# Keys x values with the values stationary in column halves, key sums by quarters of ones, and three transposes per pair

## The chip, the cores and the metric

The kernel runs on one core of a Trainium2 chip. Its time is the device time of one execution in microseconds (us); of several executions the median counts. The core's engines work side by side and wait for one another through semaphores: TensorE (PE; its weight loads are listed apart as PEld), VectorE (DVE), ScalarE (ACT), GpSimd (POOL) and SyncE (SP), which here issues most DMAs. All arithmetic is on 32-bit floats.

## The reference

A linear attention over 2 batches, 8 heads, 576 positions and 64 columns per head is followed by two blocks of wide layers. Only the attention matters here:

```
phi(x):  proj = x @ w_phi                        # 64 -> 128 features
         proj -= max(abs(proj), per row)
         return concat(exp(proj), exp(-proj))    # 256 features
q_p, k_p = phi(q), phi(k)
kv  = einsum('bhsf,bhsd->bhfd', k_p, v)          # 256 x 64 per head
z   = sum(k_p, over s)                           # 256 per head
num = einsum('bhsf,bhfd->bhsd', q_p, kv)
den = einsum('bhsf,bhf->bhs', q_p, z) + 1e-06
out = num / den
```

The result, 1152 rows of 512 columns, goes through `(x @ w_a) * (x @ w_b) @ w_out` and then through four weighted branches `relu(x @ w1[e]) @ w2[e]`.

## The kernel before, in words

The order of all work is written out by hand, as a loop over slots. In each slot every engine gets a few instructions, in program order, and an engine never passes one of its own that waits.

**Tiles.** Heads are handled in pairs, four pairs per batch. A tile is 128 rows of keys or queries of one pair; 576 rows are four full tiles and 64 rows more, so the last 64 rows of two neighbouring pairs share one mixed tile ("m"). A batch has 18 tiles, taken two at a time: nine items. There are 18 key items (slots 0 to 17) and then 18 query items (slots 18 to 35), and the loop runs some slots beyond.

**A key item** passes through three steps. `stage_proj` (L182) runs in the item's own slot: six products on PE give the projection `pj`, VectorE takes the row maxima `mx` and subtracts them (`r`, L193 and L195), ScalarE takes both exponentials (`kp`, L201 and L202). `stage_kv` (L205) runs three slots later, right after the projection of that slot. So in slots 3 to 20 PE's order is: six products of the projection, then the kv stage of the item three slots back.

**The kv stage.** For each tile and each of two heads and two signs of the exponent, 128 features of the keys are the stationary side (`lhsT`), and 128 columns are streamed: 64 columns of that head's values and 64 columns of ones, which give the key sums `z`. The tile `v` holds ones between the values of the two heads of each pair, filled by GpSimd (L142); the values are loaded around them in two DMAs per 128 rows (L151 and L155). A full tile is four products, a mixed tile eight, each over 64 rows. The sums of one pair stand in one PSUM tile `kv` of tag `nd`; when a pair is finished, VectorE (batch 0, L232) or ScalarE (batch 1, L234) copies them to `kvz`, features on the partitions.

**The query items** go through `stage_rt` (L239): four transposes on PE, exponentials on ScalarE. From slot 27 on, `stage_num` (L279) multiplies them with 32-column pieces of `kvz`: first the denominators (k = 0), then the values. `pj` and `rt` share a ring of four PSUM tiles, `num` uses the tag `nd` like `kv`.

**Around it.** Between these, ScalarE, VectorE and GpSimd prepare the weights of the later layers (`begin`, `middle`, `parts`, one step per slot from slot 5), and GpSimd and ScalarE split inputs into two parts (`xp`, L94 and L95). The rest of the kernel, from about 106 us on, is long runs of products on PE. Nothing of that is touched. `later(slot, fn)` puts a call into the list `todo`, which is emptied at the end of each slot's attention work.

Of the kernel before, what the change touches and what calls it, by code (L numbers as in the profile page):

```python
# [9 lines left out]
F32 = mybir.dt.float32  # L10
# [6 lines left out]
B, H, S, D = 2, 8, 576, 64  # L17
NP = H // 2
# [30 lines left out]
def tile_linear_attention_then_mlps(ctx, tc, qT, kT, v, w_phi, wab, wout, w12, probs, out):  # L49
    nc = tc.nc  # L50
    PSUM = bass.MemoryType.PSUM

    const = ctx.enter_context(tc.tile_pool(name="const", bufs=1, side="left"))
# [7 lines left out]
    ident = const.tile([128, 128], F32, name="ident")  # L61
    pr = const.tile([128, NTB * 3, E], F32, name="pr")
    psm = const.tile([128, NTB * 3, 1], F32, name="psm")

    hh_p = ctx.enter_context(tc.tile_pool(name="hh", bufs=1, side="left"))
    od_p = ctx.enter_context(tc.tile_pool(name="od", bufs=1, side="left"))
# [2 lines left out]
    k_p = tc.alloc_tile_pool(name="k", bufs=1, side="left")  # L69
    r_p = tc.alloc_tile_pool(name="r", bufs=1, side="right")  # L70
    nd_p = tc.alloc_tile_pool(name="nd", bufs=2, space=PSUM)
# [9 lines left out]
    with tc.manual_schedule():  # L81
# [6 lines left out]
        nc.vector.memset(wbp.bitcast(F32)[64:128, :, 0:128], 0.0)  # L88

        nc.vector.memset(psm, 0.0)  # L90
        nc.scalar.activation(out=psm, in_=psm, func=AF.Exp)

        def two_parts(hi, lo, src, eng):
# [44 lines left out]
        vt = {}  # L138

        def alloc_v(b):  # L140
            t = k_p.tile([128, 5, NP, 192], F32, tag="v", name="v", bufs=2)
            nc.gpsimd.memset(t[:, :, :, 64:128], 1.0)  # L142
            vt[b] = t

        def load_v(b, st):

            rows = v[b, st * 128:min(S, (st + 1) * 128)]
            n = rows.shape[0]
            for lo in range(0, 128, n):
                o = vt[b][lo:lo + n, st].rearrange("p a c -> p (a c)")  # L150
                nc.sync.dma_start(  # L151
                    out=o[:, 128:128 + 3 * 192].rearrange("p (a c) -> p a c", c=192)[:, :, 0:128],
                    in_=rows[:, 1:H - 1, :].rearrange("s (a h) d -> s a (h d)", h=2),
                )
                nc.sync.dma_start(  # L155
                    out=o.rearrange("p (a c) -> p a c", c=64)[:, 0:4 * NP - NP:3 * NP - 1, :],
                    in_=rows[:, 0:H:H - 1, :],
                )

        def tiles_of_batch():  # L160
            seq = []
# [9 lines left out]
        for kind in "kq":  # L171
            for b in range(B):
                for g in range(9):
                    items.append((kind, b, g, seq[2 * g:2 * g + 2]))

        st_r = {}
        st_kp = {}
        kv_ps = {}
        kvz_t = {}
# [25 lines left out]
        def stage_kv(i):  # L205
            kind, b, g, ts_ = items[i]
            kp = st_kp[i]
            done = []
            for j, t in enumerate(ts_):
                if t[0] == "m":  # L210
                    parts = [(t[1], 4, 0, 64, False, True), (t[2], 4, 64, 128, True, False)]
                else:
                    first, last = t[1] == 0, t[1] == 3
                    parts = [(t[0], t[1], 0, 128, first and t[0] % 2 == 0, last and t[0] % 2 == 1)]
                for p, st, lo, hi, first, last in parts:
                    if first:
                        kv_ps[b, p] = nd_p.tile([128, 2, 512], F32, tag="nd", name="kv")
                for h in range(2):
                    for s in range(2):
                        for p, st, lo, hi, first, last in parts:  # L220
                            c = 256 * h + 128 * s
                            nc.tensor.matmul(  # L222
                                out=kv_ps[b, p][:, 0, c:c + 128],
                                lhsT=kp[lo:hi, 2 * j + h, s, :],
                                rhs=vt[b][lo:hi, st, p, 64 * h:64 * h + 128],
                                start=first and h + s == 0, stop=last, skip_group_check=True,
                            )
                done += [(b, p) for p, st, lo, hi, first, last in parts if last]
            for b, p in done:
                t = kvz_all[:, b * NP + p]  # L230
                if b == 0:
                    nc.vector.tensor_copy(t, kv_ps.pop((b, p))[:, 0])  # L232
                else:
                    nc.scalar.copy(t, kv_ps.pop((b, p))[:, 0])  # L234
                kvz_t[b, p] = t.rearrange("p (h s f) -> p h s f", h=2, s=2)

        kvz_all = hh_p.tile([128, B * NP, 512], F32, tag="hh", name="kvz")

        def stage_rt(i):  # L239
            kind, b, g, ts_ = items[i]  # L240
# [38 lines left out]
        def stage_num(qp, kvz, k):  # L279
            t = nd_p.tile([128, 2, 512], F32, tag="nd", name="num")  # L280
            for i in range(2):
                for s in range(2):
                    for n in range(4):
                        h = n % 2
                        c = 64 * (1 - h) if k == 0 else 64 * h + 32 * (k - 1)
                        nc.tensor.matmul(  # L286
                            out=t[32 * n:32 * n + 32, i, 0:HT],
                            lhsT=kvz[n // 2][:, h, s, c:c + 32],
                            rhs=qp[n // 2][:, s, h, HT * i:HT * i + HT],
                            start=(s == 0), stop=(s == 1), tile_position=(0, 32 * n),  # L290
                        )
            return t
# [483 lines left out]
        load_chunk(0)  # L776
        load_chunk(1)
        alloc_v(0)
        load_v(0, 0)
        load_v(0, 1)  # L780
        split_x(0, nc.vector)
        high, low = ([wbp[D * g:D * g + D, k, 128 * g:128 * g + 128] for g in range(2)] for k in range(2))
# [4 lines left out]
        hi, lo = xpart[0]  # L787
# [3 lines left out]
        for st in range(2, 5):  # L791
            load_v(0, st)
# [5 lines left out]
            nc.vector.reciprocal(out=psm, in_=psm)  # L798
            nc.vector.tensor_tensor(out=pr, in0=pr, in1=psm.to_broadcast([128, NTB * 3, E]), op=ALU.mult)

        todo = {}

        def later(slot, fn, *a):
            todo.setdefault(slot, []).append((fn, a))

        def num(slot, b, half):
            pairs = [(b, 2 * half + k) for k in range(2)]
            qp = [qp_t.pop(bp) for bp in pairs]
            kvz = [kvz_t[bp] for bp in pairs]
            den = stage_den(stage_num(qp, kvz, 0))  # L810
            later(slot + 1, first, slot + 1, b, half, qp, kvz, den)

        def first(slot, b, half, qp, kvz, den):
            t = stage_num(qp, kvz, 1)
            rb = stage_rc(den)
            later(slot + 1, second, slot + 1, b, half, qp, kvz, rb, t)

        def second(slot, b, half, qp, kvz, rb, t0):
            t1 = stage_num(qp, kvz, 2)
            later(slot + 1, stage_xparts, b, 2 * half, stage_x(t0, rb))  # L820
            later(slot + 1, third, slot + 1, b, half, rb, t1)
# [9 lines left out]
        for slot in range(NI + 9):  # L831
            if slot < NI:
                kind, b, g, ts_ = items[slot]
# [12 lines left out]
            i = slot - 3  # L846
            if 0 <= i < NK:
                stage_kv(i)
            i = slot - 4
# [6 lines left out]
            if slot == 2:  # L856
                for _ in range(2):
                    load_raw()
                alloc_v(1)
                make_identity(nc, ident)  # L860
# [19 lines left out]
        for jt in order:  # L880
# [3 lines left out]
            j, tp = jt  # L884
# [65 lines left out]
```

## Time and profile before

| | us |
|---|---|
| median of 3 runs | 718.07 (717.93 to 718.54) |
| the profiled execution | 718.9 |
| its span in the trace | 717.1 |
| PE busy in the span | 709.8 |
| VectorE, GpSimd, ScalarE busy | 424.9, 309.7, 300.8 |

PE is at work almost without a break, and the chain of work that ended last runs over PE for 93% of the span. How much time a step is worth is therefore read from PE's timeline, from the start of one group to the start of the next: PE's instructions are pipelined, so the durations of neighbours overlap. The column "x16" gives the number of recorded passes; a product of 32-bit floats is recorded as two passes, a product of the projection (in a faster 32-bit form) and a transpose as one. The granted clock of PE is 1.00 in every stretch read here.

### The profile page before, as it was taken

The page shows a single profiled execution, that of the slowest core. Times are in us where ns is not written, and L with a number is a line of the kernel's source. Part 1 is how long each engine was busy: PE and PEld are TensorE (multiplying, and loading weights), DVE is VectorE, ACT ScalarE, POOL GpSimd, SP SyncE. Part 2 cuts the span into 40 slices and gives each one's busy share as a digit, 9 for nine tenths or more (in the row PEclk, how much of TensorE's full clock was granted, in tenths as well). Part 3 has the DMA queues.
Part 4 walks back from the last instruction along what each step waited for, and adds up shares of the span by engine and source line. Part 5 has one row for each costly group of instructions (what it writes and reads, how often), then busy time and mean ns, then how long its engine had stood idle before and what let it go on. Part 6 is the DMA issues. An engine that isn't in the chain of part 4 may idle for free.

```text
span 717.1 us, 12721 instructions
## 1 busy us (share of the span) xinstructions
PE 709.8 (99%) x4946; PEld 651.5 (91%) x4946; DVE 424.9 (59%) x715; ACT 300.8 (42%) x614; POOL 309.7 (43%) x294
## 2 busy tenths in 40 slices
PE   9999999999999999999999999999999999999997
PEld 8997669999999999999898989898989888888886
DVE  6879875575777764554555545554545454545454
ACT  6766665455444342233552423242324242424221
POOL 4597564244455435212555343534344334434200
PEclk9999999999999999999999999999999999999999
DMA  6775122222333330012122111211111111100003
GB/s 193 186 206 155 47 62 73 74 87 81 101 103 89 103 90 1 30 30 89 52 66 59 30 41 49 59 31 47 43 59 30 53 36 59 30 30 0 1 1 133
DMA packets 52221, 48.60 MB, mean 68 GB/s; under 512 B 8576, under 2 KB 44096, under 8 KB 52160
## 3 DMA queue, kind: packets, MB, share of 16 engines
q1 hardware_dynamic: 49344, 45.26, 21.5%
q0 software_dynamic: 2592, 2.36, 1.5%
q8 instruction: 39, 0.64, 0.4%
q14 instruction: 22, 0.18, 0.1%
q10 hardware_dynamic: 224, 0.16, 0.1%
HBM read 45.40 MB, written 2.36 MB: 67 GB/s over the span
## 4 chain that ended last, share of the span: by engine, by line
PE 93%; ACT 2%; DVE 2%; DMA 1%; SPq 1%; issue 1%; ACTq 0%; DVEq 0%
PE acc L740 9%; PE acc L739 9%; PE acc L738 9%; PE ab L658 6%; PE ab L660 6%; PE ab L659 6%; PE X L582 5%; PE X L583 5%; PE X L584 5%; PE kv L222 4%; PE num L286 3%; PE acc L689 3%; PE acc L690 3%; PE acc L688 3%; PE Z L582 2%; PE Z L583 2%
## 5 line engine op out<-in xcount | busy, mean ns | idle before, releaser
L748 DVE SCALAR_TENSOR_TENSOR oacc<-acc,pr,oacc 128x512 f32<-128x512 f32 (+1 forms) x136 | 101.5, 746 | 116.5 <-PE acc L740 116.5
L95 POOL TENSOR_TENSOR w<-wx,w 128x512 fp32r<-128x512 f32 x68 | 89.8, 1321 | 144.8 <-ACT w L94 144.8
L95 POOL TENSOR_TENSOR wc<-wt,wc 128x512 fp32r<-128x512 f32 (+1 forms) x48 | 70.1, 1487 | 113.4 <-ACT wc L94 113.4
L740 PE MATMUL acc<-w,hhb 128*128 128x512 f32 x290 | 114.2, 394 | 0.0
L658 PE MATMUL ab<-xh,w 128*128 128x288 f32 x384 | 113.5, 296 | 0.0
L739 PE MATMUL acc<-w,hhb 128*128 128x512 f32 x290 | 113.4, 391 | 0.0
L660 PE MATMUL ab<-xh,w 128*128 128x288 f32 x384 | 113.1, 295 | 0.0
L659 PE MATMUL ab<-xl,w 128*128 128x288 f32 x384 | 113.1, 294 | 0.0
L738 PE MATMUL acc<-w,hhb 128*128 128x512 f32 x290 | 112.8, 389 | 0.0
L582 PE MATMUL X<-xc,wc 128*128 128x288 f32 x256 | 77.1, 301 | 1.4 <-ACT h L587 1.4
L706 ACT ACTIVATE hhb<-h 128x288 fp32r<-128x288 f32 x64 | 36.2, 566 | 98.4 <-DVE h L590 98.4
L583 PE MATMUL X<-xc,wc 128*128 128x288 f32 x256 | 75.7, 296 | 0.0
L584 PE MATMUL X<-xc,wc 128*128 128x288 f32 x256 | 75.4, 295 | 0.0
L658 PEld LDWEIGHTS ab<-xh,w 128*128 128x128 f32 x384 | 72.0, 188 | 1.4 <-issue 1.4
L659 PEld LDWEIGHTS ab<-xl,w 128*128 128x128 f32 x384 | 72.0, 188 | 0.0
L660 PEld LDWEIGHTS ab<-xh,w 128*128 128x128 f32 x384 | 72.0, 188 | 0.0
L587 ACT ACTIVATE h<-X 128x288 f32<-128x288 f32 x64 | 26.0, 406 | 104.6 <-PE X L584 104.4
L740 PEld LDWEIGHTS acc<-w,hhb 128*128 128x128 f32 x290 | 54.4, 188 | 14.1 <-DVE hhb L707 2.9
L707 DVE SCALAR_TENSOR_TENSOR hhb<-h,hhb 128x288 fp32r<-128x288 f32 x64 | 40.5, 633 | 43.1 <-ACT hhb L706 43.1
L427 POOL TENSOR_TENSOR wx<-wx,rn 128x512 uint32<-128x512 uint32 x36 | 46.4, 1289 | 45.4 <-DVE wx L424 45.3
L739 PEld LDWEIGHTS acc<-w,hhb 128*128 128x128 f32 x290 | 54.4, 188 | 8.4
L738 PEld LDWEIGHTS acc<-w,hhb 128*128 128x128 f32 x290 | 54.5, 188 | 7.7
(105 smaller groups left out, 1614.1 us busy)
## 6 DMA issues: line engine op xcount, KB each, us to landing
raw<-in_wab SPq DMA_DIRECT2D x192, 64.0 KB, 2.1
wt<-in_w SPq DMA_DIRECT2D x64, 128.0 KB, 2.4
wx<-in_w SPq DMA_DIRECT2D x32, 256.0 KB, 3.1
raw<-in_wout SPq DMA_DIRECT2D x12, 512.0 KB, 3.7
xp<-in_qT POOLq DMA_DIRECT2D x18, 128.0 KB, 3.4
xraw<-in_qT SPq DMA_DIRECT2D x6, 384.0 KB, 3.4
out<-oacc SPq DMA_DIRECT2D x8, 256.0 KB, 2.0
xraw<-in_kT SPq DMA_DIRECT2D x5, 384.0 KB, 3.9
```

The lines of the kernel that those rows point to most:

```text
L95: eng.tensor_tensor(out=lo, in0=src, in1=hi.bitcast(F32), op=ALU.subtract)
L427: nc.gpsimd.tensor_tensor(out=x, in0=x, in1=r, op=ALU.add)
L582: nc.tensor.matmul(out=ps, lhsT=whi, rhs=xhi, start=first and a == 0, stop=False, skip_group_check=True)
L583: nc.tensor.matmul(out=ps, lhsT=whi, rhs=xlo, start=False, stop=False, skip_group_check=True)
L584: nc.tensor.matmul(out=ps, lhsT=wlo, rhs=xhi, start=False, stop=a == 1, skip_group_check=True)
L658: nc.tensor.matmul(out=t, lhsT=whi, rhs=hi, start=(c == 0), stop=False)
L659: nc.tensor.matmul(out=t, lhsT=whi, rhs=lo, start=False, stop=False)
L660: nc.tensor.matmul(out=t, lhsT=wlo, rhs=hi, start=False, stop=(c == KD - 1))
L738: nc.tensor.matmul(out=acc, lhsT=hi, rhs=whi, start=f == 0, stop=False)
L739: nc.tensor.matmul(out=acc, lhsT=hi, rhs=wlo, start=False, stop=False)
L740: nc.tensor.matmul(out=acc, lhsT=lo, rhs=whi, start=False, stop=f == 1)
L748: nc.vector.scalar_tensor_tensor(out=o, in0=acc, scalar=sc, in1=o, op0=ALU.mult, op1=ALU.add)
```

## The change

- **Loading.** `v` becomes a plain tile of whole rows, 512 columns. There is one DMA where there were two, and the fills of ones on GpSimd go. A small tile `ones` (128 x 32) is filled once.
- **kv stage.** The two sides swap. For each tile and head the 64 value columns are stationary, and the 256 features of the keys are streamed. The result stands on 64 partitions: head 0 on partitions 0 to 63, head 1 on 64 to 127 (`tile_position=(lo, 64 * h)`). The key sums are four products with `ones` as the stationary side, 32 columns wide, each in its own quarter of the columns (`tile_position=(lo, c)`), with 128 features streamed. Two pairs share one PSUM tile, one bank each.
- **Transposes.** The sums now have the features along the free side. When two pairs are finished (four times in all, in slots 7, 11, 16 and 20), ScalarE copies their 768 columns to `kt`; in the next slot `turn` transposes them on PE in six pieces, back into the same PSUM tile; in the slot after that `keep` copies them to `kvz` on ScalarE. VectorE has no copy any more.
- **num** takes its 32-column pieces at other offsets.

```diff
+    ones = const.tile([128, 32], F32, name="ones")
...
+        nc.gpsimd.memset(ones, 1.0)
...
-            t = k_p.tile([128, 5, NP, 192], F32, tag="v", name="v", bufs=2)
-            nc.gpsimd.memset(t[:, :, :, 64:128], 1.0)
-            vt[b] = t
+            vt[b] = k_p.tile([128, 5, H * D], F32, tag="v", name="v", bufs=2)
 
         def load_v(b, st):
 
             rows = v[b, st * 128:min(S, (st + 1) * 128)]
             n = rows.shape[0]
             for lo in range(0, 128, n):
-                o = vt[b][lo:lo + n, st].rearrange("p a c -> p (a c)")
-                nc.sync.dma_start(
-                    out=o[:, 128:128 + 3 * 192].rearrange("p (a c) -> p a c", c=192)[:, :, 0:128],
-                    in_=rows[:, 1:H - 1, :].rearrange("s (a h) d -> s a (h d)", h=2),
-                )
-                nc.sync.dma_start(
-                    out=o.rearrange("p (a c) -> p a c", c=64)[:, 0:4 * NP - NP:3 * NP - 1, :],
-                    in_=rows[:, 0:H:H - 1, :],
-                )
+                nc.sync.dma_start(out=vt[b][lo:lo + n, st], in_=rows.rearrange("s h d -> s (h d)"))
...
                 for p, st, lo, hi, first, last in parts:
-                    if first:
-                        kv_ps[b, p] = nd_p.tile([128, 2, 512], F32, tag="nd", name="kv")
-                for h in range(2):
+                    if first and p % 2 == 0:
+                        kv_ps[b, p // 2] = nd_p.tile([128, 2, 512], F32, tag="nd", name="kv")
+                    for h in range(2):
+                        nc.tensor.matmul(
+                            out=kv_ps[b, p // 2][64 * h:64 * h + 64, p % 2, 0:256],
+                            lhsT=vt[b][lo:hi, st, 128 * p + 64 * h:128 * p + 64 * h + 64],
+                            rhs=kp[lo:hi, 2 * j + h].rearrange("p s f -> p (s f)"),
+                            start=first, stop=last, skip_group_check=True, tile_position=(lo, 64 * h),
+                        )
                     for s in range(2):
-                        for p, st, lo, hi, first, last in parts:
-                            c = 256 * h + 128 * s
+                        for h in range(2):
+                            c = 64 * s + 32 * h
                             nc.tensor.matmul(
-                                out=kv_ps[b, p][:, 0, c:c + 128],
-                                lhsT=kp[lo:hi, 2 * j + h, s, :],
-                                rhs=vt[b][lo:hi, st, p, 64 * h:64 * h + 128],
-                                start=first and h + s == 0, stop=last, skip_group_check=True,
+                                out=kv_ps[b, p // 2][c:c + 32, p % 2, 256:384],
+                                lhsT=ones[lo:hi],
+                                rhs=kp[lo:hi, 2 * j + h, s, :],
+                                start=False, stop=last, skip_group_check=True, tile_position=(lo, c),
                             )
-                done += [(b, p) for p, st, lo, hi, first, last in parts if last]
-            for b, p in done:
-                t = kvz_all[:, b * NP + p]
-                if b == 0:
-                    nc.vector.tensor_copy(t, kv_ps.pop((b, p))[:, 0])
-                else:
-                    nc.scalar.copy(t, kv_ps.pop((b, p))[:, 0])
-                kvz_t[b, p] = t.rearrange("p (h s f) -> p h s f", h=2, s=2)
-
-        kvz_all = hh_p.tile([128, B * NP, 512], F32, tag="hh", name="kvz")
+                    if last and p % 2 == 1:
+                        done.append((b, p // 2))
+            for key in done:
+                t = kv_ps.pop(key)
+                kt = k_p.tile([128, 2, 384], F32, tag="kt", name="kt", bufs=1)
+                nc.scalar.copy(kt, t[:, :, 0:384])
+                later(i + 4, turn, i + 4, key, t, kt)
+
+        def turn(slot, key, t, kt):
+            for p in range(2):
+                for c in range(0, 384, 128):
+                    nc.tensor.transpose(out=t[:, p, c:c + 128], in_=kt[:, p, c:c + 128], identity=ident)
+            later(slot + 1, keep, key, t)
+
+        def keep(key, t):
+            o = kvz_all[:, 2 * (2 * key[0] + key[1]):][:, 0:2]
+            nc.scalar.copy(o, t[:, :, 0:384])
+            for p in range(2):
+                kvz_t[key[0], 2 * key[1] + p] = o[:, p]
+
+        kvz_all = hh_p.tile([128, B * NP, 384], F32, tag="hh", name="kvz")
...
-                        c = 64 * (1 - h) if k == 0 else 64 * h + 32 * (k - 1)
+                        c = 256 + 64 * s + 32 * h if k == 0 else 128 * s + 64 * h + 32 * (k - 1)
                         nc.tensor.matmul(
                             out=t[32 * n:32 * n + 32, i, 0:HT],
-                            lhsT=kvz[n // 2][:, h, s, c:c + 32],
+                            lhsT=kvz[n // 2][:, c:c + 32],```

The list `todo` and `later` move to an earlier place in the code, with the same text.

On PE, the kv stages that follow the projections of slots 8 and 9. The names are the outputs and inputs; "64x256 x2" is two products with 64 stationary columns and 256 streamed ones. Before:

```order
L190 MATMUL pj<-wbp,xp 128x256
L222 MATMUL kv<-v,kp 128x128 x8
L188 MATMUL pj<-wbp,xp 128x256
L189 MATMUL pj<-wbp,xp 128x256
L190 MATMUL pj<-wbp,xp 128x256
...
L222 MATMUL kv<-v,kp 128x128 x12
```

The same place now, with the first set of transposes:

```order
L187 MATMUL pj<-wbp,xp 128x256
L216 MATMUL kv<-kp,v 64x256 x2
L225 MATMUL kv<-kp,ones 32x128 x4
L216 MATMUL kv<-kp,v 64x256 x2
L225 MATMUL kv<-kp,ones 32x128 x4
L242 MATMUL kv<-ident,kt 128x128 x6
L185 MATMUL pj<-wbp,xp 128x256
```

One kind of product became an alternation of two per tile (three times in slot 9, with the mixed tile), and in slots 8, 12, 17 and 21 six transposes stand behind it.

On ScalarE, slots 7 to 9 (`kp` are the exponentials of the keys, `m`, `rn`, `w` belong to the weights, `xp` to the input three slots on). Before:

```order
L202 ACTIVATE kp<-r 128x4x128
L410 ACTIVATE m<-raw 128x512
L411 ACTIVATE rn<-raw 128x512
L94 ACTIVATE xp<-xraw 128x256
L201 ACTIVATE kp<-r 128x4x128
...
L94 ACTIVATE w<-wx 128x512
```

Now:

```order
L199 ACTIVATE kp<-r 128x4x128
L236 COPY kt<-kv 128x768
L424 ACTIVATE m<-raw 128x512
L425 ACTIVATE rn<-raw 128x512
L96 ACTIVATE xp<-xraw 128x256
L198 ACTIVATE kp<-r 128x4x128
...
L96 ACTIVATE w<-wx 128x512
...
L247 COPY kvz<-kv 128x768
```

The copy `kt` stands behind the exponentials of slot 7 and ahead of the weights' steps, and `keep` comes two slots later.

On SP, the value loads of batch 0. Two DMAs per 128 rows before:

```order
L151 DMA v<-in_v 128x3x128
L155 DMA v<-in_v 128x2x64
...
L110 DMA xraw<-in_kT 128x768
L388 DMA raw<-in_wab 32x2x256 x16
```

The same queue now:

```order
L150 DMA v<-in_v 128x512 x2
L112 DMA xraw<-in_kT 128x768
...
L402 DMA raw<-in_wab 32x2x256 x16
```

Twelve issues per batch became six, so what is queued behind them, the next chunk of keys and the first raw weights, is issued earlier.

## Rows read from the trace of the kernel before

**Rows 1.** The page: busy time by engine, and the chain's shares.

```profile
PE 709.8 (99%) x4946; PEld 651.5 (91%) x4946; DVE 424.9 (59%) x715; ACT 300.8 (42%) x614; POOL 309.7 (43%) x294
PE 93%; ACT 2%; DVE 2%; DMA 1%; SPq 1%; issue 1%; ACTq 0%; DVEq 0%
```

**Rows 2.** Stretches: bounds, length, busy time of each engine (instructions), granted clock, DMA.

```profile
8.04:54.60 46.56, 46.46 (x424) 44.99 (x423) 37.49 (x58) 31.46 (x65) 31.60 (x40) 1.00 0.73 195
54.60:64.00 9.40, 8.67 (x71) 7.76 (x69) 8.88 (x15) 6.66 (x18) 6.44 (x11) 1.00 0.62 162
```

**Rows 3.** Timeline of PE, slots 8 to 10: start, length, what.

```profile
20.67 0.36 PE L188 MATMUL pj<-wbp,xp 128*128 128x256 f32 x1
...
23.17 0.36 PE L188 MATMUL pj<-wbp,xp 128*128 128x256 f32 x1
23.37 0.28 PE L189 MATMUL pj<-wbp,xp 128*128 128x256 f32 x1
...
23.96 2.15 PE L222 MATMUL kv<-v,kp 128*128 128x128 f32 x24
26.04 0.38 PE L188 MATMUL pj<-wbp,xp 128*128 128x256 f32 x1
26.26 0.28 PE L189 MATMUL pj<-wbp,xp 128*128 128x256 f32 x1
```

**Rows 4.** Chain of waits, in order of time: kv stages of slots 4, 8.

```profile
10.80 2.21 PE kv L222 x16
...
21.62 1.79 PE kv L222 x16
```

**Rows 5.** Timeline of PE around the first num, from several narrow windows.

```profile
63.46 0.60 PE L245 MATMUL rt<-ident,r 128*128 128x128 f32 x4
63.79 0.27 PE L245 MATMUL rt<-ident,r 128*128 128x128 f32 x1
63.99 0.45 PE L286 MATMUL num<-qp,kvz 128*32 128x288 f32 x4
64.50 0.67 PE L286 MATMUL num<-qp,kvz 128*32 128x288 f32 x8
65.71 0.43 PE L286 MATMUL num<-qp,kvz 128*32 128x288 f32 x4
66.07 0.39 PE L188 MATMUL pj<-wbp,xp 128*128 128x256 f32 x1
66.29 0.28 PE L189 MATMUL pj<-wbp,xp 128*128 128x256 f32 x1
```

**Rows 6.** Groups by line: count, busy us, mean ns, idle before.

```profile
L234 ACT COPY kvz<-kv 128x512 f32<-128x512 f32 x4 | 2.3, 572 | 1.4 <-PE kv L222 1.4
L263 ACT ACTIVATE qp<-rt 128x512 f32<-128x512 f32 x24 | 13.0, 599 | 6.3 <-PE rt L245 6.2
L263 ACT ACTIVATE qp<-rt 128x256 f32<-128x256 f32 x16 | 5.2, 411 | 0.7 <-PE rt L245 0.7
L232 DVE COPY kvz<-kv 128x512 f32<-128x512 f32 x4 | 2.7, 683 | 0.6 <-PE kv L222 0.6
```

**Rows 7.** Timeline of VectorE in slots 22 to 24.

```profile
57.84 0.69 DVE L195 TENSOR_TENSOR r<-pj,mx 128x512 f32<-128x512 f32 x1
...
59.23 0.69 DVE L195 TENSOR_TENSOR r<-pj,mx 128x512 f32<-128x512 f32 x1
...
60.55 0.69 DVE L195 TENSOR_TENSOR r<-pj,mx 128x512 f32<-128x512 f32 x1
```

**Rows 8.** Timeline of PE: first projection product of slots 11, 24 and 25.

```profile
28.56 0.36 PE L188 MATMUL pj<-wbp,xp 128*128 128x256 f32 x1
...
58.63 0.35 PE L188 MATMUL pj<-wbp,xp 128*128 128x256 f32 x1 [0.72 <-PE rt L245]
...
60.02 0.36 PE L188 MATMUL pj<-wbp,xp 128*128 128x256 f32 x1
```

**Rows 9.** Timeline of ScalarE: first exponential of slot 11.

```profile
33.55 0.61 ACT L201 ACTIVATE kp<-r 128x512 f32<-128x512 f32 x1
```

More of the change, by code (lines that the diff above doesn't have):

```diff
@@ L174, in tile_linear_attention_then_mlps, with later @@
                     items.append((kind, b, g, seq[2 * g:2 * g + 2]))
+        todo = {}
+        def later(slot, fn, *a):
+            todo.setdefault(slot, []).append((fn, a))
         st_r = {}
@@ L284, in stage_num @@
                         h = n % 2
-                        c = 64 * (1 - h) if k == 0 else 64 * h + 32 * (k - 1)
+                        c = 256 + 64 * s + 32 * h if k == 0 else 128 * s + 64 * h + 32 * (k - 1)
                         nc.tensor.matmul(
                             out=t[32 * n:32 * n + 32, i, 0:HT],
-                            lhsT=kvz[n // 2][:, h, s, c:c + 32],
+                            lhsT=kvz[n // 2][:, c:c + 32],
                             rhs=qp[n // 2][:, s, h, HT * i:HT * i + HT],
@@ L799, in probabilities @@
             nc.vector.tensor_tensor(out=pr, in0=pr, in1=psm.to_broadcast([128, NTB * 3, E]), op=ALU.mult)
-        todo = {}
-        def later(slot, fn, *a):
-            todo.setdefault(slot, []).append((fn, a))
         def num(slot, b, half):
```

## The prediction

> **What bounds the kernel now.** I read the page first: TensorE (PE) is busy 99% of the span and holds 93% of the chain of work that ended last [rows 1]. So time is won or lost on PE, or where PE has to wait. The change sits in the keys' part, so I then cut out two stretches [rows 2]: 8.04 to 54.60 us (from the first kv stage to the projection of slot 21), where PE is busy 46.46 of 46.56 us and VectorE 37.49, and 54.60 to 64.00, where VectorE is busy 8.88 of 9.40 and PE only 8.67. The reader is to see there that the first stretch goes at PE's pace and the second at VectorE's. The granted clock is 1.00 in both. Last I read PE's timeline start to start, because the durations overlap.
>
> A normal slot takes 2.50 us from projection to projection [rows 3]. Its kv stage is 16 passes of 1.79 us in the chain, 0.112 each [rows 4]: every fp32 product is recorded as two passes. The six projection products take the other 0.71.
>
> **What a change of array form costs.** The new code splits the array into columns: 64-column halves for the values, 32-column quarters for the ones. The trace has two kinds of split.
> - Column quarters, at num [rows 5]. Four passes start together, one in each quarter, and the next four 0.243 us later (64.50 to 65.71 is five rounds), so the quarters run side by side. Going in: the last rt transpose starts at 63.79, the four are 0.11 apart, num starts at 63.99: 0.09 more than a step, and the first round is about 0.02 longer than the others. Coming out: the last round starts at 65.71 (its fourth pass some 0.02 later), the projection at 66.07: 0.09 more than a round; the first projection then takes 0.22 where the six together take 0.71: another 0.10.
> - Row halves, at the mixed tile. Its stage has 24 passes, but 16 of them run in pairs, so 16 steps as in a normal slot. The slot takes 2.87 us and its successor's first projection product 0.02 more than usual [rows 3]: 0.39 over 2.50, for going in and out, 0.195 each.
>
> So each change of form seen here costs 0.09 for emptying the array plus an uncovered weight load: 0.02 for 32 columns, 0.10 for 128. For 64 columns I take 0.05, between them, and keep 0.02 and 0.10 as ends.
>
> **The new kv stage.** A full tile was eight passes, 8 x 0.112 = 0.89 us. Now:
> - values: two products of 256 columns in two halves, two rounds. The round scales with the columns (0.243 for 288, 0.11 for 128): 0.216, so 0.43;
> - ones: four products of 128 columns in four quarters, two rounds of 0.11: 0.22;
> - going into halves 0.09 + 0.05 = 0.14, into quarters 0.09 + 0.02 = 0.11.
>
> Sum 0.90 us: the 0.65 of passes is shorter than 0.89, and the two changes of form take the gain away. No row shows a change from quarters to halves. It is bounded by nothing at all and by the full cost of the changes seen; below nothing is excluded, since a change of form makes no round shorter. I take the full cost, because all four changes that the rows show, in and out, rows and columns, have the same 0.09.
>
> The Trainium skill (TensorEngine Tiling, Key Properties) says that changing the tiling mode, and not just the tile, drains the TensorE. The rows agree for the changes they show; by that rule halves to quarters costs as much, which is my forecast, and without it the sum is the first rival below.
>
> A mixed tile has two row parts, each now with its own values and ones, one after the other, so it counts as two: 32 full tiles + 4 mixed x 2 = 40 pairs x 0.90 = 36.1 us. Coming out to the whole array once per kv stage: 18 x 0.19 = 3.4.
>
> **Transposes.** Per half batch six 128 x 128 transposes, 6 x 0.11 = 0.65 us of PE [rows 5]. Three of the four sets lie in the first stretch: 2.0 us. They follow the ones in whole-array form, so the change of form is already paid.
>
> **Sum over the first stretch.** 36.1 + 3.4 + 2.0 + 17 projections x 0.71 = 53.6 us, against 46.56: +7.0. The 46.56 hold some waits, such as the second kv stage, 2.21 us where 1.79 is work [rows 4]; it goes, as values are issued in half as many DMAs and PE comes later.
>
> **Slot 21 and after.** The last set stands right behind the projection of slot 21. It needs ScalarE's copy of the last sums: 768 columns, from 0.57 us for 512 and 0.19 more for another 256 [rows 6], 0.76. With some 0.2 each for the last pass to end and for the wait to clear, and 0.9 of projection and change of form beside it, PE waits about 0.25: +0.9 with the 0.65.
>
> Some comes back. Up to num at 63.99, PE needs seven projections and six sets of rt, 7 x 0.71 + 6 x 0.44 = 7.6 us, but takes 9.4: 1.8 of waiting. The longest wait ends at 58.63, when VectorE's r of 57.84 is done, the next at 60.02, after the r of 59.23 [rows 7, 8]; VectorE's beat there is 1.32 to 1.39 against PE's own 1.15. A PE that comes later finds VectorE further on, but the beat stays. I take 0.6 back, with ends 0 and 1.1.
>
> **What costs nothing.** ScalarE gets eight copies of 0.76 for four of 0.57, +3.8 us, in a stretch where it is busy 31.46 of 46.56 [rows 2, 6]; VectorE loses four of 0.68. GpSimd loses its fills of ones, SP half of its value loads. Cover: PE's stage is the longest in each slot. Behind a waiting kt copy on ScalarE stand the next slots' xp and kp, needed three slots later. If that cover goes, the third rival applies. num reads the same shapes as before, and from there PE's work is unchanged.
>
> **Total.** 7.0 + 0.9 - 0.6 = +7.3 us. The profiled execution took 718.9 us (span 717.1, 1.8 around it), so it would read 726.2; it lies 0.8 over the median of 718.07, so I predict a median of 725.4. Own range: 40 x (-0.03 to +0.05) for the 64-column load, up to 0.6 either way for what comes back: 723.4 to 728.2.
>
> **Rivals.**
> 1. *Halves and quarters follow each other without emptying the array* (not slower). Place: inside the stage. A tile costs 0.65; a normal stage 1.30 + 0.14 + 0.19 = 1.63, a mixed one three pairs, in, out, and one change between row forms, 2.43. 14 x 1.63 + 4 x 2.43 + 2.0 of transposes = 34.5, against 46.56 - 17 x 0.71 = 34.5 before: 0. The 0.9 at slot 21 falls into the 1.8 of waiting. 718.1, within 717.5 to 719.5. For it: quarters lie within halves. Against: every change seen costs 0.09. It decides if the change costs under about 0.02, at 62 changes inside the stages.
> 2. *The two halves of the values don't run side by side*, so the split does not do what it is for: 40 x 0.43 = +17.3, 742.7. Against: quarters and row halves do.
> 3. *The transposes wait for ScalarE.* In slot 11 the exponentials began at 33.55, 5.0 us after the projection at 28.56 [rows 8, 9]; with about 1.0 for the two of 0.61 that overlap and 0.76 for kt, the transposes, due 5.2 us after that projection, would wait up to 1.6: three sets, +4.8, 730.2. Against: slower slots, and VectorE without its copies, shrink the lag.
> 4. *Streaming the keys with split columns gains*: all changes of form are hidden. 14 x 1.30 + 4 x 1.96 + 2.0 = 28.0 against 34.5: -6.5, of which VectorE's pace (some 35 us of work in what would be 40, and late in places [rows 8, 9]) takes about 1.5: 713. The rows at num and at the mixed tile speak against it.
>
> The Trainium skill (TensorEngine Tiling, When to Use Tiling) proposes the swap of stationary and streaming with column tiling for 64 columns, "up to 2x"; the fourth rival is what that comes to here.
>
> **How the numbers follow.** Forecast 0.67, first rival 0.17 (0.03 of it faster, 0.11 same, 0.03 slower, if only half the cost shows), second 0.05, third 0.06, fourth 0.05. What this kernel's measurement can tell from no change is about 0.2%, 1.4 us. Faster 0.08, same 0.11, slower 0.81. The forecast's own range leaves out too much; it reaches down to the first rival and up towards the third: 717.8 to 729.5.
>
> **What would show it.** A normal slot near 2.7 us where it was 2.50, a mixed slot near 3.6 where it was 2.87; in PE's timeline about 0.3 from the last values' round to the first ones and 0.2 from the last ones to the values; transposes 0.65 per set; num first at about 71. It is wrong if a normal slot takes 2.35 (no emptying), if two values' passes start 0.2 apart (halves in series), or if PE's idle time before the transposes exceeds 0.5 in several slots.

## The result, and the profile after

The changed kernel takes 726.81 us (median of 4 runs, 726.37 to 727.10), the kernel before 718.22 beside it (717.93 to 718.54): ratio 1.0117, 95% interval 1.0104 to 1.0130. That is 8.6 us slower, where +7.3 was forecast; the median lies inside the forecast's own range of 723.4 to 728.2. The profiled execution has a span of 725.2 us, against 717.1.

The page of the changed kernel, busy time by engine and the chain of work that ended last, to be read beside [rows 1]:

```profile
PE 718.9 (99%) x5130; PEld 636.1 (88%) x5130; DVE 421.3 (58%) x711; ACT 305.5 (42%) x618; POOL 307.2 (42%) x293
PE 98%; ACT 1%; DVE 1%; issue 0%; DVEq 0%; ACTq 0%
```

PE holds 98% of the chain instead of 93%. It has 9.1 us more of busy time: the loss is PE's own work, not a wait.

The same two stretches as in [rows 2], cut at the same events (first kv stage, first projection product of slot 21, first num), columns as there:

```profile
8.00:62.82 54.82, 54.77 (x600) 29.07 (x600) 36.41 (x55) 34.64 (x67) 30.56 (x40) 1.00 0.60 173
62.82:72.44 9.62, 9.51 (x77) 8.43 (x73) 8.02 (x13) 7.66 (x19) 5.85 (x9) 1.00 0.43 112
```

The first took 46.56 and takes 54.82: +8.26. The second took 9.40 and takes 9.62: +0.22. From num to the end of the span it is 653.1 before and 652.8 after. So all of the loss lies in the keys' part, at a granted clock of 1.00, with PE busy 54.77 of 54.82. The array's weight loads (PEld) fall from 44.99 to 29.07 us there, as the swap makes the small operand stationary, and it brings next to nothing, because they lay beside PE's products: a pass of 128 streamed columns took 0.112 us before [rows 4], and a round of four takes 0.11 now, the changes of form left aside.

PE's timeline of the changed kernel, a mixed slot (slot 5) and a normal one (slot 7), to be read beside [rows 3]; columns are start, length, engine, line, operation, count:

```profile
12.65 0.39 PE L185 MATMUL pj<-wbp,xp 128*128 128x256 f32 x1
...
13.55 0.65 PE L216 MATMUL kv<-kp,v 64*64 64x256 f32 x4
14.13 0.42 PE L225 MATMUL kv<-kp,ones 64*32 64x128 f32 x8
14.49 0.65 PE L216 MATMUL kv<-kp,v 64*64 64x256 f32 x4
15.07 0.42 PE L225 MATMUL kv<-kp,ones 64*32 64x128 f32 x8
15.42 0.65 PE L216 MATMUL kv<-kp,v 128*64 128x256 f32 x4
16.00 0.43 PE L225 MATMUL kv<-kp,ones 128*32 128x128 f32 x8
16.36 0.39 PE L185 MATMUL pj<-wbp,xp 128*128 128x256 f32 x1
...
19.14 0.38 PE L185 MATMUL pj<-wbp,xp 128*128 128x256 f32 x1
...
20.05 0.65 PE L216 MATMUL kv<-kp,v 128*64 128x256 f32 x4
20.63 0.43 PE L225 MATMUL kv<-kp,ones 128*32 128x128 f32 x8
20.98 0.65 PE L216 MATMUL kv<-kp,v 128*64 128x256 f32 x4
21.57 0.43 PE L225 MATMUL kv<-kp,ones 128*32 128x128 f32 x8
21.92 0.39 PE L185 MATMUL pj<-wbp,xp 128*128 128x256 f32 x1
```

From projection to projection the normal slot takes 2.78 us (19.14 to 21.92; before 2.50) and the mixed slot 3.71 (12.65 to 16.36; before 2.87). One pair of values and ones takes 0.938 (20.047 to 20.985 in the records; 20.05 to 20.98 here) where a full tile took 0.89.

Inside that pair, from four narrow windows of the same timeline:

```profile
20.05 0.44 PE L216 MATMUL kv<-kp,v 128*64 128x256 f32 x2
20.31 0.39 PE L216 MATMUL kv<-kp,v 128*64 128x256 f32 x2
20.63 0.32 PE L225 MATMUL kv<-kp,ones 128*32 128x128 f32 x4
20.76 0.29 PE L225 MATMUL kv<-kp,ones 128*32 128x128 f32 x4
```

Each row is one round. The two halves of the values start together (x2 on one row, 0.007 us apart in the records), and so do the four quarters of the ones: the column splits run side by side, and the passes alone would need 0.65. The steps between rounds are 0.26, 0.32, 0.13 and 0.22 us where the passes are 0.216, 0.216, 0.11 and 0.11. So 0.28 to 0.29 of each pair is not passes. The steps over the two changes of form are 0.10 (halves to quarters) and 0.11 (back) longer than their passes; counted from the last pass that starts before the change, it is 0.093 both times, and the rest is the stagger of passes that start together (0.007 for two halves, 0.02 for four quarters). The first round after a change is 0.05 longer in halves and 0.025 in quarters, which fits an uncovered first weight load of 64 and of 32 columns.

The transposes, on PE at the ends of slots 8, 17 and 21, and ScalarE's copies that those of slots 8 and 17 need:

```profile
24.71 0.88 PE L242 MATMUL kv<-ident,kt 128*128 128x128 f32 x6
25.34 0.36 PE L185 MATMUL pj<-wbp,xp 128*128 128x256 f32 x1
...
52.95 0.88 PE L242 MATMUL kv<-ident,kt 128*128 128x128 f32 x6
...
63.52 0.28 PE L187 MATMUL pj<-wbp,xp 128*128 128x256 f32 x1
63.87 0.87 PE L242 MATMUL kv<-ident,kt 128*128 128x128 f32 x6
64.50 0.36 PE L185 MATMUL pj<-wbp,xp 128*128 128x256 f32 x1
```

```profile
23.30 0.78 ACT L236 COPY kt<-kv 128x768 f32<-128x768 f32 x1
...
52.12 0.78 ACT L236 COPY kt<-kv 128x768 f32<-128x768 f32 x1
```

A set takes 0.63 us from start to the next projection. At slot 8 the copy began at 23.30 and ended 0.63 before the transposes: nothing waits. The second set, at slot 12, has 1.19 to spare. At slot 17 the copy ended at 52.90, 0.05 before them, and the step from the ones to the transposes is 0.33 in the records instead of 0.20: PE waits 0.12. At slot 21 the set starts 0.35 after the last projection product, 0.23 more than its step of 0.12.

### The profile page after: what moved, and what is told of

It is laid out like the page before. It is cut to its first block, busy times and chain, and to the rows that moved or that the text cites. A ratio compares the mean times of both kernels' runs of the same rounds, so it can differ in the third digit from the quotient of the medians.

```text
span 725.2 us, 13082 instructions
## 1 busy us (share of the span) xinstructions
PE 718.9 (99%) x5130; PEld 636.1 (88%) x5130; DVE 421.3 (58%) x711; ACT 305.5 (42%) x618; POOL 307.2 (42%) x293
## 4 chain that ended last, share of the span: by engine, by line
PE 98%; ACT 1%; DVE 1%; issue 0%; DVEq 0%; ACTq 0%
PE acc L754 9%; PE acc L753 9%; PE acc L752 9%; PE ab L672 7%; PE ab L674 7%; PE ab L673 7%; PE X L596 5%; PE X L597 5%; PE X L598 5%; PE acc L703 4%; PE acc L704 4%; PE acc L702 4%; PE num L300 3%; PE kv L216 3%; PE Z L597 2%; PE Z L596 2%
```

## The experiments

Line numbers in the diffs are left out; each diff is against the changed kernel unless the text says otherwise. The kernel before, measured again beside each group of runs, took 718.22 to 718.62 us, so times of different groups compare to within 0.4 us.

### Are the changes of form the loss? Values first, then ones

All values of a stage stand ahead of all its ones, so a normal stage has two changes of form instead of four; products, tiles and sizes stay.

```
+            kept_parts = []
             for j, t in enumerate(ts_):
 ...
+                    if last and p % 2 == 1:
+                        done.append((b, p // 2))
+                kept_parts.append((j, parts))
+            for j, parts in kept_parts:
+                for p, st, lo, hi, first, last in parts:
                     for s in range(2):
 ...
-                    if last and p % 2 == 1:
-                        done.append((b, p // 2))
```

> The changed kernel (726.8 us; 8.6 above before) with one thing moved: in each kv stage all value products come first and then all products with ones, so a normal stage changes its array form twice (into halves, into quarters) where it changed four times. The work is the same. Theory (each change of form empties the array, 0.09 to 0.10 us, and leaves a weight load uncovered): a normal stage goes from 2 x 0.938 to about 1.58 us, 14 x -0.29 = -4.1; a mixed one from 2.81 to between 1.9 and 2.5, 4 x -0.3 to -0.9; in all 719 to 722. Rival (narrow products cost their time in themselves, whatever stands next to them): no change, 726.8. Rival (ScalarE's copies and the transposes are the cost): no change, 726.8.

Measured: 722.27 us (721.91 to 722.75), 4.5 under the changed kernel and 0.3 above the upper end of what was expected. PE's timeline of this kernel, a mixed slot, a normal slot and the next transposes (the bracket gives the wait before a row and what ended it):

```profile
12.88 0.39 PE L185 MATMUL pj<-wbp,xp 128*128 128x256 f32 x1
...
13.79 1.24 PE L217 MATMUL kv<-kp,v 64*64 64x256 f32 x12
14.96 0.80 PE L231 MATMUL kv<-kp,ones 64*32 64x128 f32 x24
15.70 0.38 PE L185 MATMUL pj<-wbp,xp 128*128 128x256 f32 x1
...
18.20 0.39 PE L185 MATMUL pj<-wbp,xp 128*128 128x256 f32 x1
...
19.10 1.08 PE L217 MATMUL kv<-kp,v 128*64 128x256 f32 x8
20.12 0.65 PE L231 MATMUL kv<-kp,ones 128*32 128x128 f32 x16
20.69 0.39 PE L185 MATMUL pj<-wbp,xp 128*128 128x256 f32 x1
...
23.80 0.87 PE L246 MATMUL kv<-ident,kt 128*128 128x128 f32 x6 [0.55 <-ACT kt L240]
```

The normal slot takes 2.49 (18.20 to 20.69) instead of 2.78: two changes less, 0.29 us less, 0.145 for each with its first load. The forecast had 0.14 into halves and 0.11 into quarters, 0.25 for the two. This is the price of the change of form, with all else equal. A part of the gain is lost to waits before the transposes, 0.55, 0.76 and 1.18 us at three sets.

### Does the same work without that change cost less? Values in quarters

The values are issued in four products of 32 columns, in the same form as the ones, so halves and quarters no longer alternate.

```
+                        for d in range(0, 64, 32):
+                            c = 64 * h + d
                             nc.tensor.matmul(
-                                out=kv_ps[b, p // 2][64 * h:64 * h + 64, p % 2, 0:256],
-                                lhsT=vt[b][lo:hi, st, 128 * p + 64 * h:128 * p + 64 * h + 64],
+                                out=kv_ps[b, p // 2][c:c + 32, p % 2, 0:256],
+                                lhsT=vt[b][lo:hi, st, 128 * p + c:128 * p + c + 32],
```

> The changed kernel with the values' stationary side in four quarters of 32 columns instead of two halves of 64; order as in the changed kernel. Twice as many value products, the same columns streamed per quarter; values and ones now have the same array form. Theory (changes of form): a normal stage 2 x 0.65 + 0.14 = 1.44 us against 1.88, 14 x -0.43; a mixed one about 2.2 against 2.81; in all -8.4, of which VectorE's pace may take 1: 717 to 720. Rival (narrow products cost in themselves, so more of them cost more): 32 full tiles and 8 parts with two more rounds each of 0.2 at worst, 727 to 743. Rival (copies and transposes): 726.8.

Measured: 721.15 us (720.76 to 721.39), 5.7 under the changed kernel, but just above the upper end of what was expected. PE's timeline:

```profile
17.07 0.39 PE L185 MATMUL pj<-wbp,xp 128*128 128x256 f32 x1
...
19.42 0.39 PE L185 MATMUL pj<-wbp,xp 128*128 128x256 f32 x1
...
20.32 0.64 PE L218 MATMUL kv<-kp,v 128*32 128x256 f32 x8
20.78 0.40 PE L227 MATMUL kv<-kp,ones 128*32 128x128 f32 x8
21.00 0.61 PE L218 MATMUL kv<-kp,v 128*32 128x256 f32 x8
21.43 0.40 PE L227 MATMUL kv<-kp,ones 128*32 128x128 f32 x8
23.20 0.87 PE L244 MATMUL kv<-ident,kt 128*128 128x128 f32 x6 [1.36 <-ACT kt L238]
...
34.98 0.87 PE L244 MATMUL kv<-ident,kt 128*128 128x128 f32 x6 [1.53 <-ACT kt L238]
```

A pair takes 0.67 (20.32 to 21.00): the passes and 0.02. The normal slot takes 2.35, under the 2.50 of the kernel before. So the swap does pay per tile once the form stays. What it gains is then lost elsewhere: PE is now early at the transposes and waits 1.36, 1.53 and (at 49.13) 1.56 us for ScalarE's copy. That is the wait of the prediction's third rival ("up to 1.6 us" a set), in a kernel whose slots are short enough for it.

### What do the transposes cost?

The six transposes of each set are taken out.

```
         def turn(slot, key, t, kt):
-            for p in range(2):
-                for c in range(0, 384, 128):
-                    nc.tensor.transpose(out=t[:, p, c:c + 128], in_=kt[:, p, c:c + 128], identity=ident)
             later(slot + 1, keep, key, t)
```

> The changed kernel without the 24 transposes; both copies on ScalarE stay, so the later layers get sums that stand the wrong way round. Theory: three sets of 0.63 us in the stages, 0.1 of waiting in slot 17, and 0.63 + 0.25 in slot 21, of which VectorE's pace takes part: -2.0 to -2.9, 724.0 to 724.8. Rival (transposes and the waiting for ScalarE's copies make most of the loss): -6 or more, 720 or less.

Measured: 724.79 us (724.50 to 724.90), 2.0 under the changed kernel. From slot 4 to slot 21 its trace takes 51.00 us instead of 52.95, 1.95 less: three sets of 0.63 and little else. From slot 21 to num it takes 9.35 instead of 9.62. So the fourth set, with its wait, gives back only 0.27, since without it the wait of [rows 8] is there again, on this kernel's PE timeline:

```profile
65.17 0.35 PE L185 MATMUL pj<-wbp,xp 128*128 128x256 f32 x1 [0.71 <-PE rt L256]
```

### Do the whole-row loads matter?

The values of a tile go in two DMAs again, as before the change.

```
-                nc.sync.dma_start(out=vt[b][lo:lo + n, st], in_=rows.rearrange("s h d -> s (h d)"))
+                o = vt[b][lo:lo + n, st].rearrange("p (a d) -> p a d", d=D)
+                nc.sync.dma_start(out=o[:, 1:H - 1], in_=rows[:, 1:H - 1, :])
+                nc.sync.dma_start(out=o[:, 0:H:H - 1], in_=rows[:, 0:H:H - 1, :])
```

> The changed kernel with the values loaded in two DMAs per 128 rows again (heads 1 to 6, and heads 0 and 7), so SP's queue holds twelve value loads per batch as before. Theory: PE's stages are the pace, the second kv stage begins when its values are there; 726.8, at most 0.4 more. Rival (the whole-row load gave a gain that hides part of the loss): 1 us or more above 726.8.

Measured: 727.25 us (726.97 to 727.34), ratio to the kernel before 1.0123 against 1.0117 for the changed kernel; the two intervals overlap. The difference of 0.4 us is not clear of noise, and a gain of 1 us or more from the whole-row loads, the rival, is not seen.

### Fewer ones: a miss

The ones are issued for the first tile of each pair of heads alone.

```
-                    for s in range(2):
+                    for s in range(2 if first else 0):
```

> The changed kernel with the products with ones left out of all but the first tile of each pair (8 of 40 stay), so the key sums are too small. It prices the ones and shows what paces the slots when PE gets much shorter. By PE alone a tile goes from 0.938 us to about 0.45, 32 x -0.49 = -15.6, and a normal slot to 1.92. Theory (form changes and ones are half of the stage, but VectorE with some 2.1 us per slot and the wait for ScalarE's copies take over as the pace): -8 to -12, 715 to 719, and waits of over 1 us before the transposes. Rival (PE stays the pace throughout): 711 to 712.

Measured: 721.95 us (719.74 to 722.41), not 715 to 719. PE's timeline and a stretch of the same execution (bounds, length, busy time of PE, PEld, VectorE, ScalarE, GpSimd, granted clock, DMA):

```profile
23.60 1.54 PE L242 MATMUL kv<-ident,kt 128*128 128x128 f32 x6 [3.16 <-ACT kt L236]
...
50.99 0.87 PE L242 MATMUL kv<-ident,kt 128*128 128x128 f32 x6 [2.79 <-ACT kt L236]
```

```profile
22.50:32.74 10.24, 9.14 (x47) 5.66 (x48) 5.05 (x8) 6.97 (x14) 5.14 (x6) 0.50 0.73 222
```

PE gets still earlier to the transposes and waits 3.16 and 2.79 us, and in the first of these waits the granted clock goes to 0.50, the lower of its two levels (1.2 GHz), for 10.24 us. Slots 9 and 10 then take 4.25 and 3.48 us, where slots 18 and 19, the same work at 1.00, take 2.41 and 1.92. My expectation had waits of over 1 us, but not of this length, and no fall of the clock: 5.95 us of waits and some 4 us at the lower clock are nearly all that is missing between the 15.6 us that PE alone would have gained and the 4.9 measured.

### Transposes two slots later: a miss that names the next wait

Values in quarters as above, and the transposes at slot i + 6 instead of i + 4 (diff against that kernel):

```
-                later(i + 4, turn, i + 4, key, t, kt)
+                late = min(i + 6, NK + 4)
+                later(late, turn, late, key, t, kt)
```

> The values in quarters (as in the run with quarters, 721.15) and the transposes two slots later than in the changed kernel, the last set one slot later. The quarters' trace shows PE waiting 1.36, 1.53 and 1.56 us for ScalarE's copy before three sets. Theory (those waits are the rest of the loss, the transposes themselves are filled in elsewhere): -3.5 to -4.5, 716.6 to 717.7, so level with before or just under it (718.5). Rival (the waits only move, since VectorE's late r, for which the copy queues, soon stops PE in another place): within 0.7 of 721.1.

Measured: 721.32 us (719.49 to 722.45), as without the shift, which is the rival's time but, as the rows show, not for its reason. The waits before the transposes are gone, but on PE's timeline:

```profile
33.58 0.64 PE L218 MATMUL kv<-kp,v 128*32 128x256 f32 x8 [2.75 <-ACT kvz L250]
...
35.07 0.58 PE L185 MATMUL pj<-wbp,xp 128*128 128x256 f32 x1
```

```profile
34.90:38.30 3.40, 3.40 (x34) 2.35 (x30) 1.38 (x2) 0.82 (x3) 3.38 (x5) 0.50 0.73 227
```

The transposes write back into the sums' own PSUM tile, and the keep copy of kvz (L250 here) frees it. There are two such tiles ("nd"), so the third half batch starts only when the first has been kept; the shift moved that copy behind PE's need. After the wait of 2.75 us the clock stood at 0.50 for 3.4 us. Of the nine executions the two with a mean granted clock of 1.0 took 719.49 and 719.66 us, and the seven with 0.995 to 0.998 took 720.70 to 722.45: more than 1 us of the miss goes with the clock.

The same kernel with the probabilities' load in slot 10 beside it:

> As the run before, and the load of the probabilities is issued in slot 10 where it was issued in slot 16, so that VectorE does not stand 2.3 to 3.5 us for it. Theory (VectorE, late after that wait, holds PE back before num): another -0.5 to -1.5, 715.5 to 717. Rival (PE is the pace there): no change against the run before.

Measured: 721.50 us (719.61 to 722.53): no difference, with the same wait (3.36 us at 33.68) and 6.8 us at 0.50. And that load alone, moved in the kernel before (diff against that kernel):

```
         def probabilities():
-            nc.sync.dma_start(out=pr, in_=probs)
 ...
+            if slot == 10:
+                nc.sync.dma_start(out=pr, in_=probs)
             if slot == 16:
                 probabilities()
```

> The kernel before with the load of the probabilities issued in slot 10. In its trace PE waits 1.8 us between 54.60 and 63.99, while VectorE is late after standing 3.52 us for that load. Theory: up to 1.6 comes back, 717 to 718 against 718.5. Rival (VectorE's own beat of 1.32 per slot is the limit there): no change.

Measured: 717.66 us (717.17 to 719.50), ratio 0.9986, interval 0.9977 to 0.9995: about 1 us less than the kernel before beside it (718.62). But the wait that was to go is still there. In its trace slot 21 to num takes 9.34 us instead of 9.40, with a wait of 0.71 at slot 24, and slot 20 is 0.26 shorter; the rest of the earlier num lies ahead of slot 10, where the kernels are the same. So what the move itself is worth is 0.3 us in this trace, which speaks for the rival, VectorE's beat.

### Transposes one slot later, the copy right behind them

Both waits can be met: the transposes go to i + 5, and the keep copy behind them into the same slot instead of the next, so that the PSUM tile comes free in the same slot as it did. Against the kernel with values in quarters:

```
-                later(i + 4, turn, i + 4, key, t, kt)
+                later(i + 5, turn, key, t, kt)
-        def turn(slot, key, t, kt):
+        def turn(key, t, kt):
 ...
-            later(slot + 1, keep, key, t)
+            keep(key, t)
```

> Values in quarters as in the run with quarters, the transposes of every set one slot later, and the keep copy directly behind them in the same slot instead of a slot later (so that the PSUM tile comes free no later than it did). Theory (the three waits of 1.36, 1.53 and 1.56 us before the transposes, 4.45 us together, are all that kept the run with quarters at 721.15): they go, nothing waits for the PSUM tile, the clock stays at 1.00, and the time is 716.5 to 718. Rival (the waits only move: ScalarE's keep copy, now behind the transposes of its own slot, holds the next maps or the next PSUM tile): 719 to 722, with a wait of over 1 us on TensorE in the trace.

Measured: 716.23 us (715.94 to 716.60), ratio to the kernel before 0.9970, interval 0.9959 to 0.9982, just under the lower end of what was expected. PE's timeline around the same set and at the first num:

```profile
23.01 0.64 PE L218 MATMUL kv<-kp,v 128*32 128x256 f32 x8
23.47 0.40 PE L227 MATMUL kv<-kp,ones 128*32 128x128 f32 x8
23.80 0.69 PE L218 MATMUL kv<-kp,v 64*32 64x256 f32 x16
24.25 0.45 PE L227 MATMUL kv<-kp,ones 64*32 64x128 f32 x16
24.64 0.87 PE L244 MATMUL kv<-ident,kt 128*128 128x128 f32 x6
...
61.93 2.15 PE L302 MATMUL num<-qp,kvz 128*32 128x288 f32 x32
```

No bracket stands before the transposes; num comes at 61.93, 4.66 earlier than the 66.59 of the kernel with quarters alone, which is its three waits (4.45) and little else.

This also nearly closes the account of the change. Against the changed kernel a normal slot is 0.43 shorter (2.35 against 2.78) and a mixed stage 1.18 (1.63 against 2.81): 14 x 0.43 + 4 x 1.18 = 10.7 us, where the two kernels differ by 726.81 - 716.23 = 10.6.

With the probabilities' load in slot 10 as well:

> The run before this one, and the load of the router's probabilities issued in slot 10 instead of slot 16, which took 0.6 us off the kernel before. Theory: the same gain once more, 715.5 to 717.5, so that it is the shortest of all kernels here. Rival (VectorE's wait for that load was already covered, or the waits before the transposes only move): no more than 0.2 us from the run without it.

Measured: 715.91 us (715.52 to 716.08), ratio 0.9965, interval 0.9953 to 0.9978: the shortest time here, but the two ranges overlap (715.94 to 716.60 without the move), and the difference of 0.3 us settles neither side of that expectation.

The grouped kernel with the same later transposes:

> Values first and ones behind them in each stage (two changes of form a stage instead of four), and the transposes one slot later with the keep copy directly behind. Theory (the grouped run's own waits of 0.55, 0.76 and 1.18 us before the transposes hid a part of what the saved changes of form gave): 719.6 to 720.4, that is 6.4 to 7.2 under the changed kernel. Rival (the waits go elsewhere): 721.5 to 722.5 as without it.

Measured: 719.44 us (719.01 to 719.69), ratio 1.0014, interval 1.0005 to 1.0023: 7.4 under the changed kernel and just under the lower end of what was expected, with the tile widths of values, ones and transposes all as the change has them.

## Why the prediction was right, step by step

**PE's pace.** PE was to be the bound of the first stretch throughout. It is: busy 54.77 of 54.82, and in the kernel without transposes the work of all three sets of that stretch comes off the time.

**The change of form from halves to quarters.** This was the step that no row showed, taken at the full price of the changes at num and at the mixed tile. The pair's records give 0.09 of emptying each way (0.10 and 0.11 with the stagger); the grouped kernel gives 0.145 a change with its first load, and the kernel with quarters, which has none between values and ones, loses all but 0.02 of the 0.28 over the passes. The first rival (no emptying, 718.1) and the fourth (all changes hidden, 713) fall with this. The Trainium skill's rule (TensorEngine Tiling, Key Properties) that a change of the tiling mode drains the engine holds for halves to quarters too, in both directions. The "up to 2x" that the prediction quotes at its fourth rival stands in the Trainium skill (TensorEngine Tiling) under Theoretical Speedup.

**The terms.** The pair was 0.90 and is 0.938. That is the term that was too small. The emptying of 0.09 held; what the sum left out is the stagger of passes that start together, 0.007 for two halves and 0.02 for four quarters. The prediction had seen that 0.02 at num and taken it off there, but it did not add it to the pair. The last 0.01 is rounding. Over 40 pairs it is +1.5 us, and with the transposes at 0.63 instead of 0.65 and the rest as put, 40 x 0.938 + 18 x 0.19 + 3 x 0.63 + 17 x 0.71 = 54.9, against 54.82 measured and 53.6 forecast. The exit of 0.19 and the mixed tile as three pairs hold: 3 x 0.938 + 0.19 + 0.71 = 3.71, the mixed slot to the hundredth. The range was added up loosely: its terms give 723.6 to 728.0, 0.2 inside the ends that were stated, which changes no reading.

**Halves side by side.** They start 0.007 us apart; the second rival (742.7) falls.

**Slot 21 and what comes back.** I put +0.9 and -0.6. The set costs 0.63 and a wait of 0.23, +0.86; the stretch grew by 0.22, so 0.64 came back, out of VectorE's pace as argued: the wait of 0.72 of [rows 8] is gone with the set there, and back without it.

**ScalarE's copies.** 0.78 us each against an estimate of 0.76, and all but hidden, as said. The third rival did not happen in this kernel, which fits the reason given against it, slower slots: PE comes to the first two sets 0.63 and 1.19 us after the copy has ended, and waits 0.12 at the third. It did happen in the kernels whose slots were shorter and whose transposes stood in the same place: 0.55 to 1.18 us a set in the grouped kernel, 1.36 to 1.56 in the kernel with quarters. There its three sets cost 4.45, against the +4.8 of the rival.

**Loads.** Half as many DMAs for the values were put at nothing on the path but the end of one early wait. The run with two loads agrees within 0.4 us. In it, too, slot 4 takes 2.78 us like a normal slot, so the early wait ended because PE comes later, the second of the two reasons given, and not through the number of DMAs. With whole-row loads and shorter stages a wait for the values is there again, 0.32 to 0.84 us at 11.5 to 11.7 us in five of the kernels above.

The swap's own saving is real and was in the sum (0.65 of passes for 0.89): the kernel with quarters shows it. What the change loses is the alternation of two forms, 0.28 us of each pair where the swap saves 0.24, the 2 us of transposes that the swap asks for, and a mixed tile whose two row parts no longer run together, which makes the mixed slot 0.84 longer instead of the normal slot's 0.28. That last part is the alternation too: where no change of form stands between the two parts they share their time again, in the grouped kernel with 64-column values (mixed slot 2.82, only 0.33 over its normal slot) and in quarters (the stage with its way out takes 24.64 - 23.01 = 1.63 us, where the changed kernel's mixed stage takes 16.36 - 13.55 = 2.81).

## What to carry to other kernels

Count changes of array form in PE's order before counting passes: here each cost 0.14 us, more than a 128-column fp32 pass, and an order or a tile width that keeps one form was worth 4.5 and 5.7 us of the same work, and 7.4 and 10.6 once the waits behind them were gone. When a stage is made faster, ask which copy the next stage on PE waits for and which buffer that copy frees: of the gain in quarters, 4.9 us (721.15 to 716.23) came through only when the transposes went one slot later while the copy behind them kept its slot. A swap that runs faster per tile still has to pay for what turns its result round.

## What the hardware showed beyond that

The granted clock fell to 0.50 around waits of PE of 3.16 us (fewer ones, for 10.2 us), 2.75 (transposes two slots later, for 3.4 us) and 3.36 (the same with the earlier load, for 6.8 us), so that a wait cost more than its length; the steps between projection products were then 0.21 us instead of 0.12. It did not fall around a wait of 2.79 us in the first of these kernels, nor around the waits of 1.36 to 1.56 of the kernel with quarters, and why one wait of that length was followed by it and another not stays open.

A product in a 32-column quarter was no slower here than one in a 64-column half: four values' passes of 256 columns side by side took the round of 0.22 us that two took.

In quarters, products overtook others of the same engine. In the mixed tile the code issues values, ones, values, ones for the two row parts, but the rows at 23.80 and 24.25 above show all 16 values' passes ahead of all 16 passes of ones. In the records the second part's values start 0.05 us behind the first part's, while the first part's ones, which the code issues ahead of them, start 0.45 us behind. So the sentence ahead of the prediction, that an engine never passes one of its own that waits, is too broad for TensorE's products in different rows of the array. In the changed kernel, with a change of form between, the order of the code is kept (rows at 13.55 to 15.07).
